# Four small reorderings in a fused retention and gated-FFN kernel: products around key transposes, one weight row's cast split, keys transposed inside an output block, one key transpose moved to the DMA queue

## The chip, the cores and the metric

The kernel runs on one core of one Trainium2 chip. The metric is the device time of one execution in microseconds (us), and for the kernel before it is given as the median of four runs. The profile is of one further execution, taken with the hardware profiler; it has a time of its own and a span, from the first to the last recorded instruction.

## The reference

Two stages follow each other. The first is a recurrent retention over 4 batches, 8 heads, 768 positions and a head width of 64; the second is a feed-forward part in which two projections of each token are multiplied.

```python
for t in range(S):
    state = gamma * state + einsum('bhd,bhe->bhde', k[:, :, t], v[:, :, t])
    y[:, :, t] = scale * einsum('bhd,bhde->bhe', q[:, :, t], state)
x = y.transpose(0, 2, 1, 3).reshape(B * S, H * D)      # 3072 x 512
h = (x @ w1) * (x @ w2) @ w3                           # w1, w2: 512 x 1024, w3: 1024 x 1024
out = h @ w_out                                        # w_out: 1024 x 512
```

## The kernel before, in words

All arithmetic on TensorE is in fp16 with fp32 accumulation. Nothing nonlinear stands between w3 and w_out, so the kernel first forms the product of w3 and w_out (eight tiles `W3O[f]` of 128 x 512) and then uses it as the last projection.

The sequence is cut into chunks of 128 positions; a step handles one chunk of two batches, 256 tokens, and there are 12 steps, 0 to 11. For each step the keys must stand transposed (`kT`), as must the queries (`qT`). From them come the scores `psA` (L383, or L429 in steps 0 and 1), masked on VectorE into `am` (L390, L436); the product of `am` with the scaled values (L531, L450, "intra"); the product of queries with the carried state (L599, L498, "inter"); and the state's update (L551, L467, "kv"). VectorE scales the sum into `XT`, the tokens of the feed-forward part (L614, L509). The feed-forward part runs one to two steps behind: eight pairs of an `a_unit` (x @ w1, evicted by ScalarE, L645) and a `b_unit` (x @ w2, multiplied by VectorE into `HT`, L651), four products of 256 columns each (L636), and per step two `o_unit`s of eight products of 512 columns (L661), evicted by ScalarE (L665) and stored.

The order of every engine's work is written out by hand: each engine takes its instructions in program order. The code that the change touches lies in four places.

- The start, from L734. `W3Block` forms rows 4 to 7 of `W3O`, eight products of 512 columns each (L269), cut up by `wb.mm(n)` and put between other work. `b0` and `b1` are steps 0 and 1, whose keys come as pairs of positions. `b0.k_cast` (VectorE, L735) turns the first keys to fp16, `b0.k_transposes` (L737) turns them on TensorE and copies them back with VectorE, and `b0.scores(0)` needs the copy. A scores call uses the banks X0 and X1, so the next one waits until `am_back` has emptied them.
- The weight rows, L766 to L829. The four 128-row blocks of w1 and w2 (`W1[0..3]`, `W2[0..3]`) arrive as fp32 by DMA and are cast to fp16. `W1[0]`, `W1[3]` and `W2[3]` are cast in halves, the first 512 columns by ScalarE and the other 512 by GpSimd; `W1[1]` by ScalarE alone (L775, through L220); `W1[2]`, `W2[0]` and `W2[1]` by GpSimd. `by_rows` (L789 to L794) uses them: as each row block is there, eight products of 256 columns, one for each block f of 128 columns, accumulate in four banks.
- The passage to the regular steps, L838 to L870. After the transposes of the queries of steps 2 and 3 stands the first output block, `f0.o_unit(0)`, then `k_transposes(2, "Y1")` on TensorE with a copy by VectorE (L357, L358), then the feed-forward pair `f1.ab(2)`, then in `step2` the scores of step 2, the other output block, and the pairs 3 to 7.
- The regular steps, L878 to L933. In step m the keys of step m+1 are cast (GpSimd, L303) and turned: in the steps of `K_PE = (3, 5, 8)` by TensorE ahead of pair 6 (L931, L932) with a copy by VectorE, in the others by a transposing DMA on SP's queue (`k_dma`, L362). On SP's queue the order of step m is: `k_dma(m + 1)` where there is one, the two output stores, the loads of a q tile and of k and v of step m+2, and in even steps the transposing DMAs of two q tiles (L340).

The DMAs of all loads and of most stores are issued by SP, in program order.

Of the kernel before, what the change touches and what calls it, by code (L numbers as in the profile page):

```python
# [18 lines left out]
def kernel(  # L19
# [11 lines left out]
    nc = tc.nc  # L31
# [9 lines left out]
    TB = 256  # L41
    K_PE = 4

# [64 lines left out]
    def load_rows(src, i):  # L108
        t = new_stage()
        dma_in(t[:, :], src[i * 128 : (i + 1) * 128, :])  # L110
        return t
# [19 lines left out]
    w1_st = [load_rows(moe_w1, d) for d in range(4)]  # L131
# [77 lines left out]
    W1 = [wpool.tile([128, DFF], HP, name=f"w1_{i}") for i in range(4)]  # L209
# [6 lines left out]
    def cast_to(dst, src, on_dve):  # L216
        if on_dve:
            nc.vector.tensor_copy(dst, src)
        else:
            nc.scalar.copy(dst, src)  # L220
# [16 lines left out]
    def bank(tag, shape, dtype, name):  # L237
        return ps_at.tile(shape, dtype, tag=tag, name=name)
# [41 lines left out]
    def q_cast(n, *engs):  # L280
        if n not in q_in:
            return
        q16s[n] = att.tile([128, 1024], HP, tag="q16", name="q16", bufs=2)
        pairs_cast(q16s[n], q_in.pop(n), *engs)
# [10 lines left out]
    def k_cast(m, engs):  # L295
        k16 = att.tile([128, 2, 512], HP, tag="k16", name="k16", bufs=3)
        k32 = k_in.pop(m)
        if len(engs) == 1:
            parts = [(k16[:, :, :].rearrange("p e x -> p (e x)"), k32[:, :, :].rearrange("p e x -> p (e x)"))]
        else:  # L300
            parts = [(k16[:, e, :], k32[:, e, :]) for e in range(2)]
        for eng, (dst, src) in zip(engs, parts):
            (nc.scalar.copy if eng is nc.scalar else eng.tensor_copy)(dst, src)  # L303
        k16s[m] = k16

    def v_cast(m, engs):
        v16 = att.tile([128, 2, 512], HP, tag="v16", name="v16", bufs=3)
        v32 = v_in.pop(m)
        for e, eng in enumerate(engs):
            eng.tensor_tensor(  # L310
                v16[:, e, :].rearrange("j (h d) -> j h d", d=D),
                v32[:, e, :].rearrange("j (h d) -> j h d", d=D),
                VS[:, 2, :].unsqueeze(2).broadcast_to((128, H, D)),
                MULT,
            )
        v16s[m] = v16

    def q_transposes(n, tag, on_dve):
        qTs[n] = att.tile([128, 2, NP, 128], HP, tag="qT", name="qT", bufs=5)
        pairs_transposes(qTs[n], q16s.pop(n), tag, on_dve)  # L320
# [15 lines left out]
    def q_dma(n):  # L336
        if n not in q16s:
            return
        qT = att.tile([128, 2, NP, 128], HP, tag="qT", name="qT", bufs=5)
        nc.sync.dma_start_transpose(  # L340
            qT[:, :, :, :].rearrange("p t a i -> p (t a) i"), q16s.pop(n)[:, :]
        )
        qTs[n] = qT

    def new_kT(m):
        kTs[m] = att.tile([128, 2, NP, 128], HP, tag="kT", name="kT", bufs=2)
        return kTs[m]

    def k_transposes(m, tag):
        k16, kT = k16s[m], new_kT(m)  # L350
        if tag:
            ps = bank(tag, [128, 2, NP, 128], HP, "psTk")
        else:
            ps = ps_f.tile([128, 2, NP, 128], HP, tag="psF", name="psTk")
        for e in range(2):
            for p in range(NP):
                nc.tensor.transpose(ps[:, e, p, :], k16[:, e, p * 128 : (p + 1) * 128], ident16[:, :])  # L357
        nc.vector.tensor_copy(  # L358
            kT[:, :, :, :].rearrange("p e a j -> p (e a j)"), ps[:, :, :, :].rearrange("p e a j -> p (e a j)")
        )  # L360

    def k_dma(m):  # L362
        nc.sync.dma_start_transpose(
            new_kT(m)[:, :, :, :].rearrange("p e a j -> p (e a) j"),
            k16s[m][:, :, :].rearrange("p e x -> p (e x)"),
        )
# [8 lines left out]
    def scores(m, engs=None):  # L375
        kT = kTs.pop(m)
        am = att.tile([128, 2, NP * 2, L], HP, tag="am", name="am")
        ps = [bank(f"X{r}", [128, NP * 2, L], FP, "psA") for r in range(2)]
        for e in range(2):
            for p in range(NP):  # L380
                for r in range(2):
                    for s in range(2):
                        nc.tensor.matmul(  # L383
                            ps[r][half(s), p * 2 + e, :], lhsT=kT[half(r), e, p, half(s)],
                            rhs=queries(m, e, p, s, r), start=True, stop=True,
                        )
        AMs[m] = am

        def back(r):
            nc.vector.tensor_tensor(  # L390
                am[:, r, :, :], ps[r][:, :, :],
                keep[:, :].unsqueeze(1).broadcast_to((128, NP * 2, L)), MULT,
            )

        return back

    class Pairs:
# [45 lines left out]
        def intra(self, t):  # L443
            if t == 0:
                self.y = [bank(f"Y{s}", [128, NP, 128], FP, "psY") for s in range(2)]
            for p in range(NP):
                for s in range(2):
                    for r in range(2):
                        c0 = p * 128 + r * 64
                        last = nc.tensor.matmul(  # L450
                            self.y[s][half(r), p, :], lhsT=self.v16[half(s), t, c0 : c0 + 64],
                            rhs=self.am[t][half(s), r, p, :], start=(t == 0 and p == 0),
                            stop=(s == 0 and t == 1 and p == NP - 1),
                        )
            return last
# [166 lines left out]
    class Ffn:  # L622
# [27 lines left out]
            ps = self.mm(W2, f)  # L650
            nc.vector.tensor_tensor(self.HT[:, f, :], self.pa.pop(f)[:, :], ps[:, :], MULT)  # L651

        def o_unit(self, e, parts=((0, 512),), store=True):
            bp, c = divmod(self.m, NCH)
            osb = fsb.tile([128, DM], FP, tag="osb", name="osb", bufs=4)
            r0 = (bp * 2 + e) * S + c * C if self.m > 1 else self.m * S + e * C
            for c0, c1 in parts:
                cs = slice(c0, c1)
                psO = ps_f.tile([128, c1 - c0], FP, tag="psF", name="psO")
                for f in range(8):  # L660
                    nc.tensor.matmul(  # L661
                        psO[:, :], lhsT=self.HT[:, f, e * 128 : (e + 1) * 128], rhs=W3O[f][:, cs],
                        start=(f == 0), stop=(f == 7),
                    )
                nc.scalar.activation(osb[:, cs], psO[:, :], AF.Copy, scale=final_scale)  # L665
                if store:
                    (nc.sync if self.m < NSTEP - 1 else nc.scalar).dma_start(out[r0 : r0 + 128, cs], osb[:, cs])
            return lambda: nc.sync.dma_start(out[r0 : r0 + 128, :], osb[:, :])
# [6 lines left out]
    def cast_w(W, st, d, on_dve):  # L675
        cast_to(W[d][:, :], st[d][:, :], on_dve)
# [46 lines left out]
    wb = W3Block(4)  # L723
# [5 lines left out]
    wb = W3Block(5)  # L729
# [4 lines left out]
    b0, b1 = Pairs(0), Pairs(1)  # L734
    b0.k_cast(nc.vector)  # L735
    q_transposes(0, "Y0", False)
    b0.k_transposes("Y1", True)  # L737
    b0.v_cast(nc.gpsimd, 0)
    b0.v_cast(nc.gpsimd, 1)
    wb = W3Block(6)  # L740
    wb.mm(4)
    am_back = b0.scores(0)
    am_back(0)
    am_back(1)
    wb.mm(4)
    wb.back()
    wb = W3Block(7)
    am_back = b0.scores(1)
    am_back(0)
    b0.kv(True)  # L750
# [15 lines left out]
    nc.scalar.copy(W1[0][:, 0:512], w1_st[0][:, 0:512])  # L766
    nc.gpsimd.tensor_copy(W1[0][:, 512:1024], w1_st[0][:, 512:1024])
    b1.v_cast(nc.gpsimd, 1)
    wb.mm(2)
    am_back = b1.scores(0)  # L770
    am_back(0)
    am_back(1)
    wb.mm(4)
    wb.back()
    cast_w(W1, w1_st, 1, False)  # L775
    b0.next_state_decay()
    nc.gpsimd.tensor_copy(W1[2][:, :], w1_st[2][:, :])
    nc.scalar.copy(W1[3][:, 0:512], w1_st[3][:, 0:512])
# [3 lines left out]
    f0, f1 = ffn[0], ffn[1]  # L782
# [58 lines left out]
    for f in range(2):  # L841
        f1.ab(f)
    q_transposes(3, "Y0", False)
    stores = [f0.o_unit(0, store=False)]
    k_transposes(2, "Y1")
    f1.ab(2)

    def step2():
        am_back = scores(2)
        am_back(0)  # L850
        am_back(1)
        stores.append(f0.o_unit(1, store=False))
        k_cast(3, (nc.gpsimd, nc.scalar))
        for n in (4, 5):
            q_cast(n, nc.gpsimd)
        for n in (4, 5):
            q_dma(n)
        for store in stores:
            store()
        for f in range(3, 5):  # L860
            f1.ab(f)
        intra(2)
        kv_back = kv(2, True)
        kv_back(0)
        f1.ab(5)
        k_transposes(3, None)
        f1.ab(6)
        kv_back(1)
        v_cast(3, (nc.gpsimd, nc.gpsimd))
        f1.ab(7)  # L870
# [2 lines left out]

    EARLY = (6, 11, 12)

    K_PE = (3, 5, 8)

    def step(m):  # L878

# [16 lines left out]
        if m + 1 < NSTEP:  # L896
            k_cast(m + 1, (nc.gpsimd, nc.gpsimd))
            if m not in K_PE:
                k_dma(m + 1)
# [30 lines left out]
        for f in range(4, 8):  # L930
            if f == 6 and m in K_PE:  # L931
                k_transposes(m + 1, None)  # L932
# [43 lines left out]
```

## Time and profile before

| what | value |
|---|---|
| median of four runs | 185.03 us (183.96 to 186.36) |
| the profiled execution's own time | 185.74 us |
| its span | 183.8 us |
| granted TensorE clock, mean | 0.999 |
| TensorE busy, 0 to 25 us | 21.98 us of 25.00 |
| TensorE busy, 25 to 34.3 us | 9.20 us of 9.30 |
| TensorE busy, 34.3 to 35.6 us | 0.16 us of 1.30 |
| TensorE busy, 35.6 to 52 us | 15.92 us of 16.40 |
| TensorE busy, 52 to 118 us | 66.00 us of 66.00 |
| TensorE busy, 118 to 131 us | 12.64 us of 13.00 |
| TensorE busy, 131 to 183.8 us | 49.50 us of 52.80 |
| busy over the span: VectorE, ScalarE, GpSimd | 109.4, 72.1, 70.7 us |

A matmul's record spans its whole passage through the array, so that records overlap; the distance from one start to the next is what a matmul costs TensorE in a dense stretch. In the rows of the chain of work that ended last, a row of TensorE gives that distance, summed over the matmuls that it counts: 64 matmuls of 256 columns take 6.99 us there (0.109 us each), 16 of 512 columns 3.56 us (0.22 us each), eight 128 x 128 transposes 0.45 us.

In a row of the timeline stand: start, time to the end of the last instruction merged into it, engine, line, operation, the tiles written and read, the shape, and in brackets how long the engine had been idle and what ended that. A row of SP tells of the issue of DMAs and not of their transfer; where a cast's bracket names a DMA, the cast began as soon as its data had landed.

### The profile page before, as it was taken

The numbers are of one execution on the slowest core, as the hardware profiler recorded it, in microseconds if no ns is written. First come the engines' busy times: TensorE is split into PE (matmuls) and PEld (weight loads), VectorE is DVE, ScalarE is ACT, GpSimd is POOL, SyncE is SP. The second block draws the span as 40 slices with busy tenths as digits, with TensorE's granted clock in tenths as the row PEclk, the third lists the DMA queues.
The fourth block names the chain that finished last, engine by engine and source line by source line (L and its number), as shares of the span: only waits on it lengthen the run. The fifth ranks groups of instructions, "written<-read, shape, count | busy, mean of one in ns | idle before, by whom it ended". The sixth has DMA issues, their size and how long they took to land.

```text
span 183.8 us, 6235 instructions
## 1 busy us (share of the span) xinstructions
PE 175.4 (95%) x2642; PEld 125.4 (68%) x2642; DVE 109.4 (60%) x205; ACT 72.1 (39%) x156; POOL 70.7 (38%) x126
## 2 busy tenths in 40 slices
PE   7889989799999999999999999999999999999992
PEld 2445546488757696885877858769678587685872
DVE  2338667570669678649477483495685855846330
ACT  4444746465630342433424415233244242342532
POOL 3218446664537751724426463136452160000000
PEclk9999999999999999999999999999999999999999
DMA  5999999999899999999999999969999920200203
GB/s 209 383 416 399 293 289 349 409 360 211 190 266 214 175 285 207 203 312 202 213 219 199 304 165 257 218 189 250 181 133 266 159 111 4 110 4 15 103 0 114
DMA packets 78474, 39.44 MB, mean 215 GB/s; under 512 B 56304, under 2 KB 72944, under 8 KB 78448
## 3 DMA queue, kind: packets, MB, share of 16 engines
q1 hardware_dynamic: 78016, 38.54, 87.4%
q8 instruction: 20, 0.33, 0.8%
q10 hardware_dynamic: 432, 0.52, 0.8%
q14 instruction: 6, 0.05, 0.1%
HBM read 29.36 MB, written 6.29 MB: 194 GB/s over the span
## 4 chain that ended last, share of the span: by engine, by line
PE 77%; SPq 10%; DMA 9%; ACT 2%; issue 1%; DVE 0%; ACTq 0%
PE psF L636 40%; PE psO L661 23%; SPq L63 10%; DMA stg<-in_moe_w_out_dram 4%; DMA stg<-in_moe_w_dram 4%; PE psF L791 3%; PE psY L531 2%; PE psA L383 2%; PE psY L599 2%; PE psG L636 2%; PE psK L551 2%; PE psTk L357 1%; ACT w L220 1%; PE psTq L328 0%; ACT osb L665 0%
## 5 line engine op out<-in xcount | busy, mean ns | idle before, releaser
L636 PE MATMUL psF<-xt,w 128*128 128x256 f16 x672 | 77.0, 273 | 0.0
L636 PEld LDWEIGHTS <-w 128*128 128x128 f16 x704 | 68.3, 98 | 10.3
L651 DVE TENSOR_TENSOR ht<-pa,psF 128x256 f16<-128x256 f32 x88 | 36.9, 420 | 37.3 <-PE psF L636 31.5
L645 ACT COPY pa<-psF 128x256 f32<-128x256 f32 x80 | 29.8, 372 | 38.0 <-PE psF L636 38.0
L661 PE MATMUL psO<-w3o,ht 128*128 128x512 f16 (+2 forms) x200 | 43.7, 371 | 0.0
L665 ACT ACTIVATE osb<-psO 128x512 f32<-128x512 f32 (+2 forms) x25 | 14.5, 580 | 44.9 <-PE psO L661 44.9
L661 PEld LDWEIGHTS <-ht 128*128 128x128 f16 x200 | 18.5, 98 | 19.7
L614 DVE TENSOR_TENSOR xt<-psY,YS 64x512 f16<-64x512 f32 (+1 forms) x29 | 21.1, 727 | 5.0 <-PE psY L599 4.7
L310 POOL TENSOR_TENSOR v<-stg,VS 128x512 f16<-128x512 f32 x20 | 20.5, 1042 | 5.2 <-DMA stg<-in_v_dram 5.2
L303 POOL CAST k<-stg 128x512 f16<-128x512 f32 x18 | 11.0, 612 | 23.4 <-DMA stg<-in_k_dram 23.1
L290 POOL CAST q<-stg 128x1024 f16<-128x1024 f32 (+1 forms) x12 | 12.0, 1003 | 15.8 <-DMA stg<-in_q_dram 8.2
L566 POOL TENSOR_TENSOR t<-s,GS 128x512 f16<-128x512 f32 x8 | 8.3, 1039 | 14.3 <-DVE s L565 14.3
L390 DVE TENSOR_TENSOR am<-psA,keep 128x512 f16<-128x512 f32 x20 | 12.8, 682 | 0.3 <-PE psA L383 0.2
L791 PE MATMUL psF<-xt,w 128*128 128x256 f16 x64 | 8.5, 273 | 1.3 <-ACT w L220 1.2
L248 DVE COPY w3t<-psW 128x1024 f16<-128x1024 f16 x8 | 5.5, 690 | 5.3 <-PE psW L244 5.3
L255 PE MATMUL psW<-wo,w3t 128*128 128x512 f16 x32 | 7.7, 379 | 0.8 <-ACT wo L224 0.5
L269 PE MATMUL psW<-wo,w3t 128*128 128x512 f16 x32 | 8.4, 381 | 0.0
L791 PEld LDWEIGHTS <-w 128*128 128x128 f16 x64 | 5.8, 98 | 2.9 <-ACT w L220 1.8
L684 PE MATMUL psZ<-zeros 128*128 128x512 f16 (+1 forms) x18 | 6.5, 497 | 1.3 <-DVE zeros L143 1.3
L573 DVE TENSOR_TENSOR t<-psK,t 128x512 f16<-128x512 f32 x9 | 6.2, 690 | 0.8 <-PE psK L551 0.6
L244 PEld LDWEIGHTS <-w3h 128*128 128x128 f16 x64 | 4.4, 103 | 2.9 <-DVE w3h L231 1.5
L225 POOL CAST wo<-stg 128x512 f16<-128x512 f32 x4 | 2.4, 612 | 9.7 <-DMA stg<-in_moe_w_out_dram 9.7
(90 smaller groups left out, 150.0 us busy)
## 6 DMA issues: line engine op xcount, KB each, us to landing
stg<-in_moe_w_dram SPq DMA_DIRECT2D x16, 512.0 KB, 9.4
stg<-in_q_dram SPq DMA_DIRECT2D x12, 512.0 KB, 6.3
out_dram<-osb SPq DMA_DIRECT2D x22, 256.0 KB, 3.1
stg<-in_k_dram SPq DMA_DIRECT2D x20, 256.0 KB, 5.5
stg<-in_v_dram SPq DMA_DIRECT2D x20, 256.0 KB, 5.7
stg<-in_moe_w_out_dram SPq DMA_DIRECT2D x4, 512.0 KB, 7.4
stg<-in_k_dram SPq DMA_DIRECT2D x2, 512.0 KB, 10.2
stg<-in_v_dram SPq DMA_DIRECT2D x2, 512.0 KB, 8.7
```

Source lines behind the costliest of these rows:

```text
L63: nc.sync.dma_start(dst, src)
L290: (nc.scalar.copy if eng is nc.scalar else eng.tensor_copy)(dst[:, :].rearrange("i (t h d) -> i h t d", t=2, d=D)[:, hs, :, :], src[:, :]. ...
L303: (nc.scalar.copy if eng is nc.scalar else eng.tensor_copy)(dst, src)
L310: eng.tensor_tensor(v16[:, e, :].rearrange("j (h d) -> j h d", d=D), v32[:, e, :].rearrange("j (h d) -> j h d", d=D), VS[:, 2, :].unsqueez ...
L390: nc.vector.tensor_tensor(am[:, r, :, :], ps[r][:, :, :], keep[:, :].unsqueeze(1).broadcast_to((128, NP * 2, L)), MULT,)
L614: nc.vector.tensor_tensor(XT[m][to, :, s, :].rearrange("p (a e) (i t) -> p a e t i", e=2, t=2), psYs[m][s][fr, :, :].rearrange("p (a e) (t ...
L636: nc.tensor.matmul(ps[:, :], lhsT=W[d][:, f * 128 : (f + 1) * 128], rhs=self.x(d), start=(d == 0), stop=(d == 3),)
L645: nc.scalar.copy(self.pa[f][:, :], ps[:, :])
L651: nc.vector.tensor_tensor(self.HT[:, f, :], self.pa.pop(f)[:, :], ps[:, :], MULT)
L661: nc.tensor.matmul(psO[:, :], lhsT=self.HT[:, f, e * 128 : (e + 1) * 128], rhs=W3O[f][:, cs], start=(f == 0), stop=(f == 7),)
L665: nc.scalar.activation(osb[:, cs], psO[:, :], AF.Copy, scale=final_scale)
L791: nc.tensor.matmul(ps[f // 2][:, f % 2, :], lhsT=W[d][:, f * 128 : (f + 1) * 128], rhs=f0.x(d), start=(d == 0 and f % 2 == 0), stop=(d == ...
```

## The change

Four things are moved, and nothing is computed differently.

1. Around the first keys: four products of `W3Block(6)` come ahead of `b0.k_transposes` instead of behind it, its other four between these transposes and the scores instead of behind the scores, and three products of `W3Block(7)` take the place behind the scores. The later pieces of `W3Block(7)` shrink from 1, 1, 2, 4 to 1, 1, 1, 2. The eviction `wb.back()` of block 6 is issued ahead of the two `am_back`s.
2. `W1[1]` is cast in halves by ScalarE and GpSimd. On GpSimd's queue the half stands ahead of `b0.next_state_decay` (L490).
3. `k_transposes(2, "Y1")` is issued between the fourth and the fifth of the eight products of `f0.o_unit(0)`, and `f1.ab(2)` goes behind the second output block.
4. Step 8 leaves `K_PE`: the keys of step 9 (the tenth, counting from one) are turned by a transposing DMA.

```diff
-        def o_unit(self, e, parts=((0, 512),), store=True):
+        def o_unit(self, e, parts=((0, 512),), store=True, between=None):
...
                 for f in range(8):
+                    if f == 4 and between:
+                        between()
                     nc.tensor.matmul(
...
     q_transposes(0, "Y0", False)
-    b0.k_transposes("Y1", True)
     b0.v_cast(nc.gpsimd, 0)
     b0.v_cast(nc.gpsimd, 1)
     wb = W3Block(6)
     wb.mm(4)
+    b0.k_transposes("Y1", True)
+    wb.mm(4)
     am_back = b0.scores(0)
+    wb.back()
     am_back(0)
     am_back(1)
-    wb.mm(4)
-    wb.back()
     wb = W3Block(7)
+    wb.mm(3)
     am_back = b0.scores(1)
...
-    wb.mm(2)
+    wb.mm(1)
     am_back = b1.scores(0)
     am_back(0)
     am_back(1)
-    wb.mm(4)
+    wb.mm(2)
     wb.back()
-    cast_w(W1, w1_st, 1, False)
+    nc.scalar.copy(W1[1][:, 0:512], w1_st[1][:, 0:512])
+    nc.gpsimd.tensor_copy(W1[1][:, 512:1024], w1_st[1][:, 512:1024])
     b0.next_state_decay()
...
     q_transposes(3, "Y0", False)
-    stores = [f0.o_unit(0, store=False)]
-    k_transposes(2, "Y1")
-    f1.ab(2)
+    stores = [f0.o_unit(0, store=False, between=lambda: k_transposes(2, "Y1"))]
...
-        for f in range(3, 5):
+        for f in range(2, 5):
             f1.ab(f)
...
-    K_PE = (3, 5, 8)
+    K_PE = (3, 5)
```

## The prediction

> **What bounds the kernel now.** I read the page's first line and the shares of the chain of work that ended last, then the chain in order of time, then the timeline at each place that the diff touches.
>
> ```profile
> span 183.8 us, 6235 instructions
> PE 77%; SPq 10%; DMA 9%; ACT 2%; issue 1%; DVE 0%; ACTq 0%
> ```
>
> TensorE holds 77% of the chain. What is left is the first 35 us, where transfers set the pace, and a few handovers. So a microsecond counts only if it is one that TensorE spends or stands still behind the last transfer of the start. The chain in time (start, length, what) shows where that is:
>
> ```profile
> 34.53 1.05 ACT w L220
> 35.59 0.05 issue
> 35.63 0.61 PE psF L791 x4
> ...
> 50.39 0.46 PE psTk L357 x8
> 50.85 0.02 issue
> 50.87 0.70 DVE kT L358
> 51.57 0.04 issue
> 51.62 0.45 PE psA L383 x32
> ...
> 127.81 0.45 PE psTk L357 x8
> ```
>
> Two handovers and one piece of pure TensorE work: the cast of the second w1 row, 1.05 us behind the landing of its DMA; the copy of step 2's keys, 0.70 us; and eight transposes of step 8. Before 34.5 us no work of TensorE stands in the chain, only issues and transfers. The timeline of the first passage:
>
> ```profile
> 24.25 0.62 PE L328 MATMUL psTq<-ident,k 128*128 128x128 f16 x8 [0.76 <-DVE k L290]
> 33.85 0.61 PE L791 MATMUL psF<-xt,w 128*128 128x256 f16 x4
> 34.53 1.04 ACT L220 CAST w<-stg 128x1024 f16<-128x1024 f32 x1 [1.03 <-DMA stg<-in_moe_w_dram]
> 35.84 1.04 POOL L777 CAST w<-stg 128x1024 f16<-128x1024 f32 x1 [1.74 <-DMA stg<-in_moe_w_dram]
> 37.10 0.62 ACT L778 CAST w<-stg 128x512 f16<-128x512 f32 x1 [1.52 <-DMA stg<-in_moe_w_dram]
> 37.13 0.61 POOL L779 CAST w<-stg 128x512 f16<-128x512 f32 x1 [0.25 <-DMA stg<-in_moe_w_dram]
> ```
>
> TensorE waits 0.76 us for the first keys' cast. But at 34.29 (33.85 + 4 x 0.109) it has run out of work again, until 35.63, because the weight row landed at 34.5. The rows land 1.27 us apart (34.53, 35.84, 37.10), at the pace of the transfers.
>
> **Part 1, the row products.** Four products of 512 columns are 4 x 0.216 = 0.86 us. The queries' transposes of step 0 start at 22.89 and take 8 x 0.056, so TensorE is free at 23.34; the products fill it to 24.20, and the transposes can start at 24.25 as now. VectorE's copy runs 24.91 to 25.60; the other four products run 24.71 to 25.57 beside it, and the scores start at 25.67 as now. So these 0.86 us are taken out of the time behind the scores. There TensorE waits for VectorE (second scores 26.98 and 27.46, `am` emptied bank by bank), for the value casts of GpSimd (until 27.49), for the second keys (30.01), and last for the w1 row. None of these moves. The gap at 34.29 only grows. Value 0; the landing at 34.5 hides it. Bounds: a late start of the transposes by 0.05 is swallowed by the same gap, and if the landing came 0.86 us sooner, all 0.86 would be gained. I take 0.
>
> **Part 2, w1's second row in halves.** A 512-column half is 0.62 us on ScalarE (37.10) and 0.61 on GpSimd (37.13), against 1.04. GpSimd is idle at 34.53 (its decay L490 ran 33.49 to 34.10). TensorE resumes at 34.53 + 0.62 + 0.05 = 35.20, not 35.63: gain 0.43. Behind the half on GpSimd's queue waits the decay of b0's state, 0.61 us, now 35.14 to 35.75; the next cast, L777, starts at its landing, 35.84, and is not touched; the decay's reader comes at 57 us. What is late next: `W1[2]` is cast at 36.88 and was read at 37.71, now 37.28; `W1[3]` at 37.74, read now at 38.14; the first block of w2 has half a microsecond. `W2[2]` follows TensorE itself (ScalarE evicts `pa`, casts, TensorE waits), so it moves along. q of step 3 is cast at 47.08 and is read now at 47.62. All slack is over 0.2, so 0.43 passes. Bounds: 0 if a later landing takes it, 0.83 if W1[2]'s whole slack were usable, which nothing here does.
>
> **Part 3, keys of step 2 inside the output block.** Now: transposes 50.22, copy 50.87 to 51.56, scores 51.62; the pair `ab(2)` covers TensorE only to 50.67 + 0.44 = 51.11, so 0.51 is idle. After, in the same times: block from 48.50, four products to 49.36, transposes to 49.81, four products to 50.67; the copy starts 0.65 behind the transposes' start (as 50.22 to 50.87 now), 50.01 to 50.70, scores 50.76. Idle 0.09, gain 0.42. VectorE is free (it idled 1.82 before that copy). The key halves that the transposes read: ScalarE's half ends at 48.90 now, about 48.7 after part 2, because it then starts at its landing just after 48.0; the transposes start at 49.36 - 0.43 = 48.93. The pair `ab(2)` goes behind the second block: same length. Behind it the update of step 2 needs a bank that the second block's eviction frees (0.60 of ScalarE), about 0.8 before it is asked for. Bounds: 0, if key or copy is late, to 0.51.
>
> **Part 4, keys of step 9 by the queue.** Removed from TensorE: the row of 0.45 at 127.81, in a stretch where it never waits (48 + 16 matmuls around it at 0.109). Removed from VectorE: one copy, 0.69, off the chain. Added on SP: one transposing DMA ahead of the stores of step 8.
>
> ```profile
> 119.25 0.61 POOL L303 CAST k<-stg 128x512 f16<-128x512 f32 x1 [1.61 <-DMA stg<-in_k_dram]
> 117.64 1.15 SPq L63 DMA_DIRECT2D stg<-in_q_dram  x1
> 121.50 2.08 SPq L667 DMA_DIRECT2D out_dram<-osb  x2
> ```
>
> ```profile
> L363 SPq DMA_TRANSPOSE kT<-k x5: 1238/1330/2329, 74.5 to 143.5; - x5
> DMA to landing us min/median/max: 3.1/4.7/5.1
> ```
>
> The first fence is of the timeline; the second of the view of L363, time on SP in ns and from issue to landing. The keys are cast at 119.86. SP is idle from 118.79 to 121.50, so it issues at 119.9 and is done by 121.2 to 122.2; it lands at 123.0 to 125.0. The scores of step 9 start at 130.47, minus 1.3 by the sum below: 129.2. Slack 4.2 us. Moved past it on SP: two stores (up to 0.7 later; their buffers are asked for again two steps on), then one q tile and the k and v loads of step 10, which in the present run start at 123.64, after both stores. They start when the second store has its data, about 0.8 earlier than now, so the transpose is out of the way. Gain 0.45. If the loads were late after all, step 10's keys have 142.36 - 1.3 = 141.1 against an issue at 133.93 and 5.1 to land: 2.0 us.
>
> Here two rules speak. The Trainium skill, "DMA: Bandwidth & Descriptors", section "Latency and other measured facts", gives DMA transposes 261 GB/s. From it I estimate 256 KB / 261 = 1.0 us of all 16 DMA engines, and the page's DMA row stands at 9 in most slices of the first 140 us: by the rule every later load lands 1.0 us later, and step 10's keys keep 1.0 of their 2.0 us, still a gain of 0.45. The other, "TensorE: Matmul & The Clock Gate", section "Part 4: PE-mode transpose", gives about 275 ns for one transpose and says that the fast clock does not engage for it. Eight would be 2.2 us and the whole change -3.05. The row says 0.45 for eight, since they overlap; I take the row.
>
> **Sum.** 0 + 0.43 + 0.42 + 0.45 = 1.30. Span 183.8 - 1.3 = 182.5; the profiled execution's own 185.74 lies 1.94 outside its span, so it would be 184.4. That execution is 0.71 above the median; on the median, 185.03 - 1.30 = 183.7.
>
> **Rivals.**
> - Transfers take part of it back. From 34 to about 50 us casts begin at landings (the brackets above), and part 2 uses up slack of which the keys' half keeps only 0.2. If part 2 is lost the time is 184.2, if parts 2 and 3, 184.6. Against: every slack counted above is positive.
> - More than the sum: at 118.30 the chain has 0.35 of "issue", in which TensorE waits for nothing that the profile shows. If that doesn't recur in the new program, 183.4; with half of part 1's bound as well, 183.0. For: part 1 does free TensorE earlier. Against: nothing removes the landing at 34.5.
> - Slower: the DMA transpose holds SP. If the keys of step 9 land late, SP stands still ahead of two stores, the q tile and four loads, and step 10's scores wait for their keys. It begins to cost at 2.0 us of delay, and all 1.3 are gone at 3.3; at 5 us it is 185.03 - 1.3 + 3.0 = 186.7. Against: SP is idle for 2.7 us just there, and k loads land 5.5 us from their issue (median of the page's DMA issues).
> - Part 4 without effect (TensorE waits for the same 0.45 elsewhere): 184.2; it falls in the first case's range.
>
> **Chances.** The sum as worked out 0.62 (183.2 to 184.2 by itself); partly taken back 0.22 (184.2 to 185.0); more 0.11; slower 0.05. The runs of before spread over 2.4 us, so a median of a few can be off by some 0.5, and about 1% (1.85 us) is what a measurement of this kernel can tell from no change. Faster by over 1% means below 183.18: the third case and a fifth of the first, 0.23. Slower by over 1%: 0.04. The rest 0.73. Range 182.8 to 185.0.
>
> **What would show it.** Part 1: scores still at 25.67, and a wider gap ahead of the w1 row. Part 2: two casts of about 0.62 at 34.5 and TensorE at 35.2; wrong if `W1[2]` then stops it. Part 3: less than 0.2 us ahead of step 2's scores, near 50.3. Part 4: four rows of L358 instead of five, six transposing DMAs of keys, and no wait at step 9's scores. The prediction is wrong if TensorE's idle time grows after 35 us, above all at steps 9 and 10.

## The result, and the profile after

The changed kernel takes 184.00 us in the median of 29 runs (182.81 to 186.34), the kernel before 184.68 us in 48 (183.83 to 186.38). The ratio is 0.9947, with a 95% interval from 0.9928 to 0.9965: 0.98 us less, by the interval 0.65 to 1.33. The ratio is that of the means without slow runs, those over 1.5% above the fastest of their kernel (two of the 29, none of the 48); the medians alone differ by 0.68. A second set of runs gave 0.9945 [0.9923, 0.9967]. The forecast of -1.30 us lies inside the interval, at its far end. The profiled execution took 184.02 us, against 185.74 before.

The page's first line and the shares of the chain, after:

```profile
span 182.3 us, 6220 instructions
PE 78%; SPq 10%; DMA 8%; ACT 1%; issue 1%; ACTq 0%
```

The span is 1.5 us shorter. ScalarE's share of the chain has fallen from 2% to 1%, and VectorE is no longer in it. The same chain in order of time (start, length, what):

```profile
35.23 0.61 PE psF L795 x4
...
49.12 0.45 PE psTk L357 x8
49.57 0.86 PE psO L663 x4
50.43 0.38 PE psA L383 x32
...
117.49 0.12 issue
...
121.52 6.99 PE psF L636 x64
128.51 0.37 PE psY L531 x32
```

And of the chain before, in step 8:

```profile
118.30 0.35 issue
...
122.57 5.24 PE psF L636 x48
127.81 0.45 PE psTk L357 x8
128.25 1.75 PE psF L636 x16
```

Before, the row's products began at 35.63, the copy by VectorE stood between transposes and scores of step 2, and the 64 products of step 8 were cut in 48 and 16 by eight transposes. Now TensorE runs from transposes through products to scores without a break, and the 64 are in one piece. The same landmarks in both chains, where the names are the same:

| landmark | before | after | gained so far |
|---|---|---|---|
| first products of w1's second row | 35.63 | 35.23 | 0.40 |
| products of masked scores (L531), step 2 | 54.77 | 53.95 | 0.82 |
| the same, step 7 | 117.22 | 116.41 | 0.81 |
| output block of step 8, behind an "issue" of 0.35 and 0.12 | 119.01 | 117.96 | 1.05 |
| L531, step 8 | 130.00 | 128.51 | 1.49 |
| last eviction | 180.75 | 179.21 | 1.54 |

So in this pair of executions part 2 gave 0.40, part 3 0.42, part 4 0.44, and part 1 nothing. The 0.23 between steps 7 and 8 belongs to no part: it is a stall of TensorE that was shorter this time. Without it the last evictions differ by 1.3.

The timeline of the start, after (idle time and what ended it in brackets):

```profile
24.61 0.62 PE L328 MATMUL psTq<-ident,k 128*128 128x128 f16 x8
26.02 0.42 PE L429 MATMUL psA<-qT,kT 64*64 64x128 f16 x16
34.56 0.62 ACT L778 CAST w<-stg 128x512 f16<-128x512 f32 x1 [1.33 <-DMA stg<-in_moe_w_dram]
34.59 0.61 POOL L779 CAST w<-stg 128x512 f16<-128x512 f32 x1 [0.82 <-DMA stg<-in_moe_w_dram]
35.23 0.61 PE L795 MATMUL psF<-xt,w 128*128 128x256 f16 x4 [0.68 <-ACT w L778]
```

Part 1 is in the first row: before, TensorE had idled 0.76 us for VectorE's cast ahead of these transposes, and now no wait stands there. The scores behind them, forecast at 25.67, came at 26.02, because this time VectorE began the keys' cast, at the landing, at 23.86 and not at 23.50. That part 1 is worth nothing here is in the last row: the row of w1 began its cast at 34.56 as at 34.53 before, and TensorE waits for it again. The two halves take 0.62 and 0.61 us side by side, as worked out.

The view of L363 and, of SP's timeline, the stretch around part 4:

```profile
L363 SPq DMA_TRANSPOSE kT<-k x6: 1239/1642/2083, 74.1 to 142.6; - x6
```

```profile
119.07 2.00 SPq L363 DMA_TRANSPOSE kT<-k  x1
121.17 1.37 SPq L669 DMA_DIRECT2D out_dram<-osb  x2
```

Six transposing DMAs instead of five. The new one is issued at 119.07 and landed 4.6 us later, at 123.7; its reader starts at 129.05 without a wait. The stores behind it go out at 121.17, before at 121.50. They are not later, but they gave something up: the first of them had its data at 120.43, when the eviction ended, and stood 0.74 us behind the transposing DMA on SP's queue. The forecast had allowed for up to 0.7.

### The profile page after: what moved, and what is told of

Same layout as the page of the kernel before. It is cut to its first block, busy times and chain, and to the rows that moved or that the text cites. A ratio compares the mean times of both kernels' runs of the same rounds, so it can differ in the third digit from the quotient of the medians.

```text
span 182.3 us, 6220 instructions
## 1 busy us (share of the span) xinstructions
PE 174.9 (96%) x2634; PEld 125.0 (69%) x2634; DVE 108.7 (60%) x204; ACT 71.7 (39%) x156; POOL 71.4 (39%) x127
## 4 chain that ended last, share of the span: by engine, by line
PE 78%; SPq 10%; DMA 8%; ACT 1%; issue 1%; ACTq 0%
PE psF L636 41%; PE psO L663 23%; SPq L63 10%; DMA stg<-in_moe_w_out_dram 5%; DMA stg<-in_moe_w_dram 4%; PE psF L795 3%; PE psY L531 2%; PE psY L599 2%; PE psA L383 2%; PE psG L636 2%; PE psK L551 2%; PE psTk L357 1%; ACT w L220 1%; PE psTq L328 0%; ACT osb L667 0%
```

## The experiments

The theory of the forecast: each part removes one handover or one piece of TensorE's work, at the size that the profile of before shows, and the parts add up. Its rivals: one part does it all or takes from another; the transfers at the start, which land when they land, eat what is gained ahead of them; keys turned by the queue arrive late at some step. All ratios below are to the kernel before, with their 95% interval. One microsecond is 0.0054.

**Each part alone.** Four kernels, each the kernel before with one part of the change.

```diff
 part 1:  b0.k_transposes, wb.mm and wb.back in the changed order
 part 2: -    cast_w(W1, w1_st, 1, False)
         +    nc.scalar.copy(W1[1][:, 0:512], w1_st[1][:, 0:512])
         +    nc.gpsimd.tensor_copy(W1[1][:, 512:1024], w1_st[1][:, 512:1024])
 part 3: +    o_unit(0, ..., between=lambda: k_transposes(2, "Y1"))
 part 4: -    K_PE = (3, 5, 8)
         +    K_PE = (3, 5)
```

> The kernel before with part 1 alone, the row products around the first keys' transposes. Theory A (each part is worth the handover or the TensorE work that it removes, and the parts add up): 0.0 us, with TensorE stopped about 0.86 us longer ahead of the second w1 row's products, which begin near 35.6 us as before. Rival B (freeing TensorE early is what carries the gain): -0.4 to -0.9 us. Rival C (a share of the gain is chance, namely in the stretch of 0.35 us in step 8 in which TensorE waits for nothing that the profile shows): 0.0, but with that stretch shorter than 0.35.

Measured: 0.9999 [0.9969, 1.0029], nothing, as expected; the interval reaches to -0.57 us, so the smaller gains of rival B are not excluded. The way there was not the expected one. Timeline:

```profile
32.70 0.61 PE L792 MATMUL psF<-xt,w 128*128 128x256 f16 x4 [0.50 <-ACT w L767]
33.31 1.04 ACT L220 CAST w<-stg 128x1024 f16<-128x1024 f32 x1 [0.17 <-DMA stg<-in_moe_w_dram]
```

The second row came over a microsecond earlier than in the profile of before, and TensorE hardly stopped for it. What part 1 saves went into a wait of 0.50 us for the first row.

> The kernel before with part 2 alone, the second w1 row cast in halves. Theory A: -0.43 us, the row's first products near 35.2 instead of 35.63, and the lead still there in step 2. Rival B: nearly nothing alone, since TensorE is not free any earlier. A further rival (later transfers take the lead back): -0.43 at 35 us, and 0 behind the keys of step 2, near 50 us.

Measured: 0.9999 [0.9974, 1.0024]. That is 0 with half a microsecond either way, and less than expected. Rival B (nothing alone, since TensorE is not free any earlier) gives the same number, but not for its reason: in the profile of before, without part 1, TensorE stood at this row for over a microsecond, so it was free.

> The kernel before with part 3 alone, step 2's keys transposed inside the first output block. Theory A: -0.42 us; scores of step 2 near 50.8, with under 0.15 us of idle time ahead of them instead of 0.5. Rival (the copy or the cast of the keys is late without part 2 in front): 0 to -0.2 us, with TensorE waiting for the copy.

Measured: 0.9982 [0.9952, 1.0011], -0.33 us. The gap ahead of the scores of step 2 is gone, but this profile shows something else. Two rows of the waits (engine, tile, line, for what, us in total, times, longest):

```profile
PE psA L383 <- DMA kT<-k: 1.8, 2, 0.9
PE psA L383 <- DMA qT<-q: 0.5, 1, 0.5
```

In steps 5 and 8 TensorE waited 0.9 us each for keys that the queue turns in both kernels, and 0.5 in step 4 for queries. These DMAs are no part of the change.

> The kernel before with part 4 alone, step 9's keys by a transposing DMA. Theory A: -0.45 us, TensorE's eight transposes gone and no wait at step 9's scores. Rival (the DMA holds SP and delays the loads behind it): 0 or slower, with step 10's keys landing over 2 us later than before. Rival C: -0.45, and if the unexplained 0.35 us of step 8 is gone as well, -0.8.

Measured: 0.9984 [0.9960, 1.0008], -0.30 us; no wait at step 9's scores. Step 10's keys went out at 133.69 (133.93 before), so the new DMA did not make them late.

No part alone can be told from nothing, and together their ratios come to -0.7 us, each with about 0.5 us of uncertainty, the sum with about 1. For sizes, then, rows of the profile have to serve. Those of parts 3 and 4 repeat from execution to execution. For part 3 take the distance from the last transposes of queries ahead of step 2 to step 2's masked scores' product, in the timelines of before and after:

```profile
48.05 0.61 PE L328 MATMUL psTq<-ident,q 128*128 128x128 f16 x8
54.70 0.45 PE L531 MATMUL psY<-am,v 64*64 64x64 f16 x32
```

```profile
47.65 0.61 PE L328 MATMUL psTq<-ident,q 128*128 128x128 f16 x8
53.88 0.45 PE L531 MATMUL psY<-am,v 64*64 64x64 f16 x32
```

These are 6.65 and 6.23 us. The distance is 6.64 or 6.65 in all five profiles without part 3, and 6.23 to 6.27 in seven of the nine with it (6.36 and 6.42 in two of the kernels below, the second at a lower clock). Part 4 is as steady: in the chain, the products of step 8 take 5.24 + 0.45 + 1.75 us in all six profiles whose kernel turns step 9's keys on TensorE, and 6.99 in one piece in seven of the eight others (7.20 in the one at a lower clock).

The rows of part 2 differ from execution to execution. Its own profile, timeline:

```profile
33.49 0.62 ACT L775 CAST w<-stg 128x512 f16<-128x512 f32 x1
33.87 1.29 DVE L436 TENSOR_TENSOR am<-psA,keep_t 128x512 f16<-128x512 f32 x2 [0.64 <-PE psA L429]
34.01 1.05 PE L792 MATMUL psF<-xt,w 128*128 128x256 f16 x8
34.99 0.64 PE L450 MATMUL psY<-am,v 64*64 64x128 f16 x16
```

And that of part 4 alone, where the row is still cast whole:

```profile
33.47 1.05 ACT L220 CAST w<-stg 128x1024 f16<-128x1024 f32 x1
33.77 1.29 DVE L436 TENSOR_TENSOR am<-psA,keep_t 128x512 f16<-128x512 f32 x2 [0.47 <-PE psA L429]
33.93 1.26 PE L791 MATMUL psF<-xt,w 128*128 128x256 f16 x8
35.12 0.42 PE L450 MATMUL psY<-am,v 64*64 64x128 f16 x16
```

In both the cast starts at 33.5 with no bracket: the row had landed before ScalarE came to it, about a microsecond earlier than in the profile that the forecast was read from. The whole cast ends at 34.52, and TensorE hardly stops: its eight products take 1.26 us instead of 1.05. These 0.21 are given back at once. The products of the masked scores come next; with halves they take 0.64 us for 16, with the whole cast 0.42, and end at 35.63 and 35.54. VectorE's masks are ready at 35.16 and 35.06 (33.87 and 33.77, each + 1.29), and TensorE cannot get far ahead of them. In both, the third row's products begin 3.9 us after those of the first row; in the profiles of before and after it was 5.0 and 4.5. So with an early landing part 2 is worth next to nothing, and VectorE sets the pace.

**The change and the kernel before once more.** Is the landing a matter of the kernel or of the execution? Both kernels again, unchanged; the kernel before ran a single time.

> The kernel before, unchanged, for a second profile of the same program. Theory E (when the second w1 row lands differs from one execution to the next, and with it what part 2 is worth): the row may land near 33.3 instead of 34.5 us; if it does, TensorE's stop of 1.2 us ahead of its products shrinks to under 0.3 us and the first output block starts near 47.6 instead of 48.5. Rival (the landing belongs to the program or to the other chip): 34.5 us again within 0.2, and a stop of 1.2 us. A look alone: one execution can show that it varies, not how often.

The profile, timeline:

```profile
33.77 0.61 PE L791 MATMUL psF<-xt,w 128*128 128x256 f16 x4 [1.04 <-ACT w L766]
34.39 1.04 ACT L220 CAST w<-stg 128x1024 f16<-128x1024 f32 x1 [0.19 <-DMA stg<-in_moe_w_dram]
```

The second row is late again (34.39), as the rival has it, but now the first row is late as well: TensorE stops there, for 1.04 us, and has no stop of note at the second row, against the rival. A third form of the same start.

> The changed kernel, unchanged, timed again and profiled a second time beside the next two. The change as a whole: a ratio of 0.993 to 0.997 to the kernel before. Theory E: the second w1 row lands at 33.3 to 34.6; the first output block starts at 47.5 to 48.1 with it. The waits of the scores for a DMA of keys or queries: none or up to 2 us, differing from execution to execution.

Measured: 0.9945 [0.9923, 0.9967]. The profile, timeline and then waits:

```profile
33.21 0.62 ACT L778 CAST w<-stg 128x512 f16<-128x512 f32 x1
```

```profile
PE psA L383 <- DMA kT<-k: 0.6, 2, 0.4
```

The same program, and the cast starts at 33.21 instead of 34.56. The two profiles may be of different chips. But the kernels below that change only `K_PE` have the same start, ran on the same chip as this one, and cast this row at 33.06 to 34.77 (the two kernels after them, with the same start, at 34.48 and 33.42), the latest being:

```profile
34.77 0.62 ACT L778 CAST w<-stg 128x512 f16<-128x512 f32 x1 [0.88 <-DMA stg<-in_moe_w_dram]
```

So the landing differs from execution to execution. And this execution waits in steps 5 and 8 for keys, which the first profile of the same program did not.

Over all 14 profiles of this study (12 experiments, before and after) the cast of this row starts at 33.7 or earlier in nine and at 34.3 or later in five. TensorE stopped at the second row to the full size (1.17 us) in the profile of before; with halves it still stopped there in two (0.68 in the change, 0.23 in the kernel with K_PE = (5,) below). In the other two late ones the first row was late too, and the stop was there.

**The change without part 1.**

```diff
-    wb.mm(4)
-    b0.k_transposes("Y1", True)
-    wb.mm(4)
+    b0.k_transposes("Y1", True)
     (and the other wb calls as in the kernel before)
```

> The changed kernel without part 1, the row products where they were before. Theory A (part 1 is worth nothing whatever the rest does, because VectorE's masked scores and the landing of the row set when TensorE goes on): within 0.2 us of the changed kernel. Rival B (part 1 pays once part 2 has shortened the wait behind it): 0.3 to 0.5 us slower than the changed kernel.

Measured: 0.9965 [0.9942, 0.9988], 183.98 us in the median against 184.05 for the whole change on the same chip. By the ratios that is 0.4 us slower than the whole change, by the medians 0.07 faster, and the difference of the ratios is uncertain by 0.6. So time alone does not exclude rival B's 0.3 to 0.5. The rows do not support them: the first row's products began at 32.51 here, and in the five profiles with part 1 and an early second row at 32.4 to 32.8.

**How much slack do the keys have?** Three kernels vary only K_PE in the changed kernel, the list of steps in which TensorE still turns the keys.

```diff
-    K_PE = (3, 5)
+    K_PE = (3,)                        first
+    K_PE = (5,)                        second
+    K_PE = (3, 4, 5, 6, 7, 8, 9, 10)   third
```

> The changed kernel with step 5 taken out of K_PE as well, so that step 6's keys are also turned by the queue. Theory A (TensorE's work alone counts): -0.45 us against the changed kernel. Theory D (the queue is near its limit; what SP issues later lands later, and TensorE gives time back at the scores): between -0.2 and +1 us, because this DMA is issued behind two others of q, near 88 us, lands near 92 to 93, and is needed near 93.0; in some executions TensorE waits for the keys at step 6.

Measured: 0.9956 [0.9924, 0.9988]. One more step by the queue, and no wait in the profile (issue at 86.66, earlier than expected). But its time cannot be told from that of the change (0.9945 on this chip), and its runs reach from 182.67 to 187.44.

> The changed kernel with step 3 taken out of K_PE instead, so that step 4's keys are turned by the queue. Theory A: -0.45 us against the changed kernel. Theory D: slower by 0.3 to 1.5 us, since the DMA can be issued only behind two of q and two stores, near 65.5 us, lands near 70, and is needed at 69.1; TensorE waits for it at step 4's scores, and the loads behind it are late by about 1 us too.

Measured: 1.0223 [1.0158, 1.0288], +4.1 us to the kernel before and about 5.1 to the changed kernel, in six runs. The timeline, issue and reader:

```profile
67.10 1.29 SPq L363 DMA_TRANSPOSE kT<-k  x1
71.84 0.45 PE L383 MATMUL psA<-qT,kT 64*64 64x64 f16 x32 [1.71 <-DMA kT<-k]
```

Here is the wait of the slower rival: 4.7 us from issue to the scores, of which TensorE stood still 1.71. That accounts for less than half of the loss. The other part visible is the granted clock: 0.948 in this execution and 0.978 to 0.991 in its five others, where no run of the kernels above is below 0.989; the 64 products of a step take 7.20 us, not 6.99, which is 3% more. The profiled execution's span is 5.9 above that of the change. As an estimate from these rows, 1.7 of it is the wait and 3% of the 147 us behind the start, 4.4, the clock, less 0.45 for the transposes that are gone: 5.7. So the 4.1 is not the price of the queue alone. Why this kernel had the lower clock, no run shows.

> The changed kernel with all keys from step 4 on turned on TensorE and none by DMA: six times eight transposes more on TensorE. Theory A: +2.7 us (6 x 0.45) against the changed kernel, and runs as scattered as before (2.4 to 3.7 us between the fastest and the slowest). Theory D (in many executions the keys' DMA lands late and TensorE waits): +1.2 to +2.3 us, and runs scattered by less than 2 us, since nothing waits for a DMA of keys any more.

Measured: 1.0200 [1.0126, 1.0274], +3.7 us to the kernel before and about 4.7 to the changed kernel, more than either theory gave, and times from 187.13 to 192.07 in six runs. The scatter didn't go down, so the times scatter without the transposing DMAs of keys too. The profiled execution is the shortest one, with a span of 185.4: 3.1 above the change. Of this 1.43 is one stop, in the timeline:

```profile
131.80 0.22 PE L599 MATMUL psY<-qT,t 64*64 64x64 f16 x3 [1.43 <-issue]
```

The rest, 1.7 net of what else differs between two executions, is less than six times 0.45 = 2.7. What the longer executions lose was not profiled and stays open.

**Two more steps along the same way.** At about 43 us TensorE waits for the third w2 row (its weight loads stand still for 0.38 in both kernels). In the first kernel GpSimd casts it, behind `W2[1]`; in the second `K_PE = (3,)` is added.

```diff
+    nc.gpsimd.tensor_copy(W2[2][:, :], w2_st[2][:, :])
     ...
-    cast_w(W2, w2_st, 2, False)
```

> The changed kernel with the third row of w2 cast by GpSimd behind the second, instead of by ScalarE behind an eviction. In all profiles so far TensorE is stopped for about 0.26 us (0.37 from start to start instead of 0.11) at this row, near 43 us, whatever the landings. Theory A (each handover removed is a gain): -0.26 to -0.36 us, the stop gone. Theory D (the landing of step 2's keys, near 48 us, sets what follows): 0 to -0.1, with TensorE stopped ahead of step 2's keys instead.

Measured: 0.9936 [0.9908, 0.9964], 183.73 us; the stop at 43 us is gone, and the distance from the third w1 row's products to the last query transposes falls from 10.34 to 10.07 us. The lowest ratio of the study, but its interval covers the ratio of the change.

> The changed kernel with the third row of w2 cast by GpSimd and step 6's keys turned by the queue, the two additions that did not make it slower by themselves. Theory A (adds up): 0.26 + 0.45 = 0.7 us faster than the changed kernel. Theory D (the keys' DMA has no slack left in some executions): 0 to 0.4 us faster, runs more scattered than those of the changed kernel.

Measured: 0.9969 [0.9934, 1.0004], 0.4 us slower than the change by the ratios, with intervals that overlap, and not 0.7 faster. The timeline, issue and reader in step 8:

```profile
112.57 1.28 SPq L363 DMA_TRANSPOSE kT<-k  x1
117.93 0.45 PE L383 MATMUL psA<-qT,kT 64*64 64x64 f16 x32 [1.60 <-DMA kT<-k]
```

TensorE waits 1.60 us, in a step whose keys the queue turned in every kernel but the one without key DMAs. In the profile of before this DMA was issued at 110.46, 2.1 us earlier, and nothing waited.

This issue sorts the profiles. Step 8's keys were issued between 109.8 and 111.1 us in seven profiles without a wait of TensorE for them, at 111.9 in one where they landed as they were needed, and between 112.6 and 113.9 in the four in which TensorE waited 0.4 to 1.6 us. (`(5,)` is apart, being late as a whole, and the kernel without key DMAs has none.) So the queue ran late in these executions before this DMA was issued; why, no run shows.

## Why the prediction was right, point by point

- **Part 1, 0.** Right, and in the profiled pair for the reason given: the row of w1 lands at its time. Alone it measured 0.9999, within 0.6 us. The bound beside it was wrong: "if the landing came 0.86 us sooner, all 0.86 would be gained". In five profiles with part 1 it did come sooner, and in three of them TensorE then waited 0.3 to 0.5 us for the first row; behind that, VectorE's masks set the pace.
- **Part 2, 0.43.** Right for the execution that it was read from (0.40), and mis-sized for the median. The forecast took the landing at 34.5 for a property of the kernel. It is one of several outcomes: a stop that halves shorten by 0.43 stands in three of 14 profiles. In the others the first row, the third row or VectorE's masks are last and the halves bring about 0. Weighted so, as an estimate, the term is 3/14 x 0.43 = 0.1, and the sum 0 + 0.1 + 0.42 + 0.45 = 0.97, against 0.98 measured. So close a match is luck: 14 profiles of 12 kernels are few, the medians differ by 0.68 only, and the interval (0.65 to 1.33) holds the 1.30 too. What is shown is the mechanism, the size of the mean is an estimate.
- **Part 3, 0.42.** Right: 0.42 in the landmarks and in the other profiles, and no gap ahead of scores that start at 50.4 (50.3 was expected).
- **Part 4, 0.45.** Right: 0.44 in the landmarks, the DMA landed in 4.6 us against 3.1 to 5.1 taken, with 5.3 us left (4.2 were counted), and no load went out later. Step 10's keys, issued at 133.37 and read at 140.82, keep 2.4 us by the forecast's reckoning (2.0 were counted). So the loss of 1.0 us of this slack that the forecast estimated from the 261 GB/s of the Trainium skill, "DMA: Bandwidth & Descriptors", section "Latency and other measured facts", is not seen. Nor are the 2.2 us for eight transposes from the 275 ns of "TensorE: Matmul & The Clock Gate", section "Part 4: PE-mode transpose": the 64 products joined up 0.45 shorter, as the row had it.
- **Left out of the prediction: the slack of the other steps.** It followed the new DMA into step 9 and the loads of step 10, but not the keys that were already on the queue. In the profile of before, step 5's were issued at 74.50 and needed at 81.64; they took 5.0 us to land, which leaves 2.1, and step 8's, issued at 110.46, needed at 117.68 and landed in 3.1, had 4.1. Five of 14 profiles show TensorE waiting there or, with `K_PE = (5,)`, at step 4, 0.6 to 1.8 us in all. One of the two profiles of the changed kernel is among them, and none of the two of the kernel before, but part 1 alone, which touches no queue, is. The DMA that part 4 adds is issued at 119, behind both, so it cannot delay them; whether the other parts make such waits more frequent cannot be told from so few.
- **The rivals.** "More than the sum" came true in the profiled pair through the very stall of 0.35 that it named (0.12 after), but such a stall comes and goes between executions (0.03 in the second profile of the kernel before), so it is no gain of the change. "Slower": its mechanism is real at step 4 (1.71 us of wait), where the keys have less time, and did not occur at step 9, where SP was idle as counted. "Partly taken back": the median of 184.00 lies in the range of the plain sum (183.2 to 184.2), but in what happened this rival is the nearest. Part 2 is missing in most of the profiles, not by used-up slack but because there is nothing for it to remove.

## What to carry to other kernels

A handover that the profile shows behind a landing is worth its size only in executions where that landing is last; profile the same program two or three times before crediting it. Before one more transfer is put on a queue, list the slack of every transfer that is on it already, and look at it in more than one execution: the same transfer had 4 us to spare in one and came late in another. Parts of 0.4 us in 184 cannot be told singly by time (intervals of about 0.5 us either way). Distances between landmarks that do not depend on what landed before them show such parts, to 0.05 us here, if stalls that belong to no part are set aside.

## What the runs showed of the hardware that was not expected

- The second w1 row's cast started at 34.56 and at 33.21 in two executions of one program, and over the profiles the wait moved between the first row, the second row and VectorE accordingly.
- The stop called "issue" (0.35 before, 0.12 after) stands behind the same number of TensorE's instruction records, 3521 matmuls and weight loads, in three kernels. In the kernel with `K_PE = (5,)`, where eight transposes ahead of it are gone, 19 of the 32 products of L599 come before it instead of 12, so it goes with the count and not with the instruction. In the kernel without key DMAs one of 1.43 us stands 512 records further on, and in the kernel with part 4 alone one of 0.31 us 2048 records earlier. The page's DMA table has a queue of 20 packets, named "instruction", besides those of the data. That the engine waits for the next piece of its program fits this, but it is inferred, and no run took it away.
- One kernel on one core ran at a granted clock of 0.948 over its whole span, and its other executions at 0.978 to 0.991.
